# Fifteen small loads and eight early output stores on ScalarE's queue, in a decode kernel for gated attention and MLP

## The chip, the cores and the metric

The kernel runs on one core of a Trainium2 chip. The metric is the device time of one launch in microseconds (us): 1326.11 is the median of two runs before the change (1326.09 and 1326.12). The names of the engines are those of the profile: PE is TensorE (matmuls), DVE is VectorE, ACT is ScalarE, POOL is GpSimd, SP is SyncE, which here only issues DMAs. "SPq" and "ACTq" are the instructions with which SP and ACT issue DMAs.

## What is computed

Two rows (a batch of 2, one new token each) pass through attention over a cache of 16384 positions and, beside it, through a mixer with an MLP. A gate of each row mixes the two:

```python
g = sigmoid((x * gate_w).sum(-1, keepdims=True))
a = attention(x, k_cache, v_cache, wq, wo)     # B=2, 32 heads, Sk=16384, Dh=128
b = mixer_mlp(x, w1, w2, w3, w4)               # D=1024, F=3584
return g * a + (1 - g) * b                     # [2, 1, 1024], bf16
```

In the mixer a sequence of length 1 is shifted by one or two positions, so the operand of w2 is zero, and w1 isn't needed; the kernel multiplies a zeroed tile by w2. What has to be read is almost all cache: K and V are 2 x 32 x 16384 x 128 bf16 each, 268 MB apiece, of 570 MB in all.

## The kernel before

**The ring.** All large operands pass through one on-chip buffer, `ring`, of five slots, each 128 partitions by 32 KB. A K or V block of two heads takes two slots (8.4 MB), a half of a weight takes one. SP issues every one of these loads in one fixed order: wq (two halves, slots 0 and 1), w2 (slot 2), w3 (two halves, slots 3 and 4), w4 (two halves, slots 0 and 1 again), then K and V in turn for 32 pairs of heads (K in slots 3 and 4 or 2 and 3, V in 0 and 1), and wo at the end. Ahead of each load SP waits until the last matmul that reads the slot's earlier content is done; SP's queue is in order, so a load that waits holds those behind it.

**The prologue.** Each engine has one instruction list, emitted in program order. A wait is on a semaphore, and an instruction that waits holds all behind it on its engine. The steps ahead of the loop over head pairs are these:

- ACT loads the rows of x (L560) and of the gate vector (L561) into `xg_row`, and then, once POOL has cleared the tile `xrow`, x again into `xrow` in four pieces of two rows, at partitions 0 and 1, 32 and 33, and so on (L563). `xrow` is read at the end of the MLP only (L511).
- PE transposes `xg_row` (L583), and multiplies by wq (L604), which frees slots 0 and 1. DVE copies q out (L609, L616).
- The gate stage: DVE multiplies and sums (L393, L396), PE sums over partitions (the helper at L389), ACT takes a tanh (L399, preceded by ACT's table load), and DVE makes the gate and its complement from it (L400 to L406).
- The w2 stage: PE (L495), DVE (L531), PE (L537); DVE adds x (L481); the layer norm on DVE and PE, with one instruction on POOL (L430), gives `xn_bf` (L432).
- w3: 112 matmuls on each half (L466). The last of them frees slots 3 and 4, and SP may issue the first K load (L349).
- The gelu on DVE (L442 to L450) with a tanh on ACT (L448), then w4 on PE (L495), 56 matmuls for each half. The end of the second half frees slots 0 and 1 for the first V load (L353). DVE adds `xrow` and scales (L511, L513).

**The loop.** For each of the 32 pairs DVE transposes K in the ring (L647), PE makes the scores (L653), a softmax follows on DVE, PE and ACT (L663 to L680), PE multiplies by V (L689), and the result goes into a small tile (L698 to L703). Each pair's last reads of a slot release the next load into it.

**The end.** PE multiplies by wo (L726), DVE copies the two output rows into `orow` (L750), and SP and ACT store one row each (L752), and wait until it has landed.

`pl.dma(engine, fn, sem, waits)` puts a DMA on an engine's list and gives the event of its landing; `pl.add(engine, fn, waits)` puts any other instruction there.

Of the kernel before, what the change touches and what calls it, by code (L numbers as in the profile page):

```python
# [9 lines left out]
BF16 = mybir.dt.bfloat16  # L10
# [110 lines left out]
def build_kernel(nc, A_x, A_k, A_v, A_wq, A_wo, B_w1, B_w2, B_w3, B_w4, gate_w, out, dbg=None):  # L121
    dbg = dbg or {}
    B, Sq, D = A_x.shape
# [4 lines left out]
    P = 128  # L128
# [10 lines left out]
    NBD = D // P  # L139
# [19 lines left out]
    NQ = 4  # L159
    DQ = D // NQ  # L160
    PR = 32 * (NQ - 1) + 2
    assert DQ <= 512

    with ExitStack() as st:
        block = st.enter_context(nc.Block())
        sb = lambda name, shape, dt: st.enter_context(nc.sbuf_tensor(name, shape, dt))
# [34 lines left out]
        xrow = sb("xrow", [P, DQ], BF16)  # L201
        bgrow = sb("bgrow", [P, DQ], F32)
        orow = sb("orow", [P, DQ], BF16)
        m24 = sb("m24", [P, 2, NQ], F32)
        m2 = sb("m2", [P, 2], F32)
        gm = sb("gm", [P, 2], F32)
# [16 lines left out]
        sem = lambda n: st.enter_context(nc.semaphore(n))  # L223
# [3 lines left out]
        s_gw = sem("dgw")  # L227
        s_out = [sem(f"dout{i}") for i in range(2)]
        s_xr = sem("dxr")
        s_tail = [sem(f"dtl{i}") for i in range(len(wo_runs[1]))]  # L230
        pl = _Plan(esems)

# [37 lines left out]
        for hp in range(HP):  # L270
# [7 lines left out]
                    waits=(ev_rowm,), sig=True)  # L278
# [4 lines left out]
                        waits=(e0,), sig=True)  # L283
# [56 lines left out]
        def q_load(key):  # L340
            queue_load(key, wloads[key], (w_slots[n_w[0]],))
            n_w[0] += 1
# [219 lines left out]
        for qd in range(NQ):  # L562
            ev_xr = pl.dma("act", lambda e, qd=qd: e.dma_start(xrow[32 * qd:32 * qd + 2, :], A_x[:, 0, qd * DQ:(qd + 1) * DQ]), s_xr,  # L563
                           waits=(ev_xr0,))
        for hi in range(2):
            q_load(("wq", hi))
        for key in w_order:
# [14 lines left out]
        for nb in range(NBD):  # L582
            last = pl.add("pe", lambda e, nb=nb: e.transpose(tr_ps[:, nb * 4:nb * 4 + 3], xcols(xg_row, 3, nb), ident[0:3, 0:3]),  # L583
                          waits=(ev_x, ev_gw, ev_ident), sig=(nb == NBD - 1))
# [27 lines left out]
        for bp in range(NBP):  # L612
            evp = pl.add("pe", lambda e, bp=bp: e.matmul(q4_ps[:, bp, :], lhsT=PermQ[:, bp, :],
                                                        rhs=q_sb[:, :, :].rearrange("p h b -> p (h b)"), start=True, stop=True),
                         waits=(ev_q, ev_const, ev_r0), sig=(bp == NBP - 1))
# [135 lines left out]
        for b, eng in enumerate(("sp", "act")):  # L751
            ev_out = pl.dma(eng, lambda e, b=b: e.dma_start(out[b, 0, :].rearrange("(q n) -> q n", q=NQ), orow[b:PR:32, :]), s_out[b],  # L752
                            waits=(ev_fin,))
# [28 lines left out]
def bass_gated_mix__mha_block_cached__mixer_s_mlp__decode_kernel(  # L782
    nc: bass.Bass,
    A_x: bass.AP,
    A_k_cache: bass.AP,
    A_v_cache: bass.AP,
    A_wq: bass.AP,
    A_wo: bass.AP,
    B_x: bass.AP,
    B_w1: bass.AP,  # L790
    B_w2: bass.AP,
    B_w3: bass.AP,
    B_w4: bass.AP,
    gate_w: bass.AP,
    out: bass.AP,
):
    build_kernel(nc, A_x, A_k_cache, A_v_cache, A_wq, A_wo, B_w1, B_w2, B_w3, B_w4, gate_w, out)
# [28 lines left out]
```

## Time and profile before

| | |
|---|---|
| median of the two runs | 1326.11 us |
| the profiled execution's own time | 1325.93 us |
| its span, first to last instruction | 1324.1 us |
| PE busy | 785.1 us (59%) |
| DVE busy | 657.2 us (50%) |
| ACT busy | 45.7 us (3%) |
| DMA traffic | 570.60 MB, mean 431 GB/s |

One execution was recorded by the hardware profiler. Times in its views are counted from the start of the span. A row of the timeline has the start, the busy time, the engine, the line of the kernel, the operation, the tiles written and read, and the count of instructions that were merged into the row; in brackets stands how long the engine had been idle and what ended that. A row of the waits has the waiting line, the line waited for, the total, the count and the longest. A row of a DMA queue has its packets, megabytes, and the time that its packets took as a share of the 16 DMA engines' time in the window asked for (packets are counted by their starts, so a short window can show over 100%). q1 and q10 are the queues of SP and of ACT.

### The profile page before, as it was taken

Reading aid. Unit: us, or ns where it says so; the run is one execution under the profiler, and the core shown is the slowest. Engines: PE = TensorE matmul, PEld = TensorE weight load, DVE = VectorE, ACT = ScalarE, POOL = GpSimd, SP = SyncE. Lnnn points to the kernel's source line nnn. Section 1 sums busy time; section 2 is a strip of 40 time slices with the busy share of each in tenths; the row PEclk is TensorE's granted clock in tenths of the full one; section 3 lists DMA queues with packets and bytes.
Section 4 is the critical chain, followed back from the end, with each engine's and each line's share of the span. In section 5 each row is a group of like instructions: output and inputs, shape, how many; then the busy total and the mean of one; then the engine's idle time right before and its main releaser. Section 6 shows DMA issues by size and latency. Waiting matters only on the chain.

```text
span 1324.1 us, 12290 instructions
## 1 busy us (share of the span) xinstructions
PE 785.1 (59%) x5235; PEld 335.8 (25%) x5235; DVE 657.2 (50%) x523; ACT 45.7 (3%) x99; POOL 23.5 (2%) x110
## 2 busy tenths in 40 slices
PE   3645557656556765555676555566655456665646
PEld 2512223222222322222232222222222222222223
DVE  1054446655444665544466554446655444665543
ACT  0000000000000000000000000000000000000000
POOL 3000000000000000000000000000000000000000
PEclk9966787777678777767877776788787788878679
DMA  9999999999999999999999999999999999999998
GB/s 403 445 424 434 436 434 434 432 438 432 430 440 432 430 440 430 430 440 430 434 436 430 438 434 436 432 432 438 434 428 440 432 430 440 430 432 438 430 434 359
DMA packets 11138, 570.60 MB, mean 431 GB/s; under 512 B 1252, under 2 KB 1268, under 8 KB 1655
## 3 DMA queue, kind: packets, MB, share of 16 engines
q1 hardware_dynamic: 11096, 570.43, 99.7%
q8 instruction: 8, 0.13, 0.0%
q10 hardware_dynamic: 30, 0.01, 0.0%
q14 instruction: 4, 0.02, 0.0%
HBM read 570.44 MB, written 0.00 MB: 431 GB/s over the span
## 4 chain that ended last, share of the span: by engine, by line
DMA 70%; PE 23%; DVE 6%; issue 0%; SPq 0%
DMA ring<-in_A_k_cache_dram 65%; PE ps L653 23%; DVE ring L647 6%; DMA ring<-in_B_w_dram 3%; DMA ring<-in_A_wo_dram 2%; PE ps L466 1%; SPq L324 0%; DVE orow L750 0%; PE ps L726 0%
## 5 line engine op out<-in xcount | busy, mean ns | idle before, releaser
L653 PE MATMUL ps<-ring,Z 128*128 128x512 bf16 x2048 | 534.5, 420 | 389.1 <-DVE ring L647 388.5
L647 DVE STREAM_TRANSPOSE ring<-ring 128x2048 f32<-128x2048 f32 x256 | 565.2, 2275 | 278.6 <-DMA ring<-in_A_k_cache_dram 278.6
L653 PEld LDWEIGHTS ps<-ring,Z 128*128 128x128 bf16 x2048 | 204.4, 104 | 706.7 <-issue 473.5
L689 PE MATMUL ps<-ring,PT_sb 128*32 128x512 bf16 x2048 | 168.2, 501 | 4.1 <-DVE recip L680 3.7
L703 DVE SCALAR_TENSOR_TENSOR OT_sb<-ps,gT,recip 128x2 f32 x32 | 7.0, 220 | 203.4 <-PE ps L700 203.4
L689 PEld LDWEIGHTS ps<-ring,PT_sb 128*32 128x32 bf16 x2048 | 67.6, 122 | 90.8 <-issue 69.6
L674 ACT ACTIVATE P_sb<-ps,negm 128x512 bf16<-128x512 f32 x32 | 22.0, 687 | 1013.9 <-DVE negm L672 1013.9
L663 DVE TENSOR_REDUCE rA<-ps 128x1 f32<-128x512 f32 x32 | 22.1, 692 | 64.1 <-PE ps L653 64.1
L678 PE MATMUL ps<-rowsum,hsel 128*128 128x1 f32 x128 | 24.0, 291 | 37.9 <-ACT P_sb L674 37.9
L676 DVE STREAM_TRANSPOSE PT_sb<-P_sb 128x512 bf16<-128x512 bf16 x32 | 22.8, 711 | 27.0 <-ACT P_sb L674 27.0
L634 POOL TENSOR_TENSOR Z<-q_f,mask 128x8 bf16<-128x8 f32 x64 | 12.3, 227 | 1214.3 <-PE ps L653 1214.3
L678 PEld LDWEIGHTS ps<-rowsum,hsel 128*128 128x128 f32 x128 | 21.3, 236 | 40.7 <-ACT P_sb L674 40.7
L665 PE MATMUL ps<-ident,rmax_bf 128*1 128x128 bf16 x32 | 6.9, 217 | 33.1 <-DVE rmax_bf L664 33.1
L698 ACT ACTIVATE acc_sb<-ps 128x512 bf16<-128x512 f32 x32 | 19.1, 597 | 198.8 <-PE ps L689 198.8
L700 PE MATMUL ps<-dsel,acc_sb 128*128 128x2 bf16 x128 | 8.1, 167 | 22.5 <-ACT acc_sb L698 22.5
L466 PE MATMUL ps<-xn_bf,ring 128*128 128x2 bf16 x224 | 14.5, 202 | 2.9 <-DMA ring<-in_B_w_dram 2.9
L466 PEld LDWEIGHTS ps<-xn_bf,ring 128*128 128x128 bf16 x224 | 14.4, 172 | 3.0 <-DMA ring<-in_B_w_dram 3.0
L700 PEld LDWEIGHTS ps<-dsel,acc_sb 128*128 128x128 bf16 x128 | 5.3, 96 | 38.2 <-ACT acc_sb L698 38.2
L665 PEld LDWEIGHTS ps<-ident,rmax_bf 128*1 128x1 bf16 x32 | 2.5, 79 | 48.9 <-DVE rmax_bf L664 48.9
L604 PE MATMUL ps<-xT_bf,ring 128*128 128x2 bf16 x256 | 7.1, 165 | 11.7 <-DVE xT_f L588 7.4
L666 DVE TENSOR_REDUCE m_sb<-ps 1x2 bf16<-1x128 bf16 x32 | 8.9, 278 | 9.9 <-PE ps L665 9.9
L672 DVE TENSOR_SCALAR negm<-ps,cAB 128x1 f32<-128x1 f32 x32 | 8.9, 277 | 9.2 <-PE ps L669 9.2
(97 smaller groups left out, 85.8 us busy)
## 6 DMA issues: line engine op xcount, KB each, us to landing
ring<-in_B_w_dram SPq DMA_DIRECT2D x4, 3584.0 KB, 35.4
ring<-in_A_wq_dram SPq DMA_DIRECT2D x2, 4096.0 KB, 17.5
ring<-in_A_wo_dram SPq DMA_DIRECT2D x1, 4096.0 KB, 40.2
ring<-in_B_w_dram SPq DMA_DIRECT2D x1, 2048.0 KB, 27.1
ring<-in_A_wo_dram SPq DMA_DIRECT2D x1, 2048.0 KB, 22.2
ring<-in_A_wo_dram SPq DMA_DIRECT2D x1, 1024.0 KB, 24.4
ring<-in_A_k_cache_dram SPq DMA_DIRECT2D x32, 26.8
ring<-in_A_v_cache_dram SPq DMA_DIRECT2D x32, 29.2
```

What stands on the lines that cost most here:

```text
L466: fn = lambda e, nb=nb, kl=kl: e.matmul(out_ps[:, nb, :], lhsT=cols(wv, kl, nb, nout), rhs=rhs_of(k0 + kl), start=False, stop=True, skip_g ...
L634: ev = pl.add("pool", lambda e, hp=hp: e.tensor_tensor(Z[:, :, ZO:ZO + P].rearrange("p t (i c) -> p t i c", c=32)[:, :, 2 * hp:2 * hp + 2, ...
L647: return pl.add("dve", lambda e: e.transpose(ap, ap), waits=(arrived(("k", n)),), sig=True)
L653: ev = pl.add("pe", lambda e, bp=bp: e.matmul(S_ps[:, 0:NCOL], lhsT=Z[:, bp, ZO - 2 * u:ZO - 2 * u + P], rhs=kv[:, :, bp // 2, :, bp % 2], ...
L663: e1 = pl.add("dve", lambda e: e.tensor_reduce(rA[:, :], S_ps[:, 0:NCOL], axis=AX.X, op=ALU.max), waits=(ev_S[n],), sig=True)
L665: e3 = pl.add("pe", lambda e: e.transpose(mt_ps, rmax_bf[:, :], ident[:, :]), waits=(e2,), sig=True)
L674: e7 = pl.add("act", lambda e: e.activation(P_sb[:, :], S_ps[:, 0:NCOL], ACT.Exp, bias=negm[:, 0:1], scale=scale, accum_out=rowsum[:, 0:1] ...
L676: e8 = pl.add("dve", lambda e: e.transpose(PT_sb[:, :], P_sb[:, :]), waits=(e7,), sig=True)
L678: e9 = pl.add("pe", lambda e, hp=hp: e.matmul(l_ps[:, hp:hp + 1], lhsT=hsel[:, hp, :], rhs=rowsum[:, 0:1], start=True, stop=True, skip_gro ...
L689: ev = pl.add("pe", lambda e, jj=jj, cg=cg: e.matmul(acc_ps[32 * cg:32 * cg + 32, 0:512], lhsT=PT_sb[:, 32 * jj:32 * jj + 32], rhs=vv[:, 4 ...
L698: e1 = pl.add("act", lambda e: e.activation(acc_sb[:, :], acc_ps[:, 0:512], ACT.Copy), waits=(ev_pv,), sig=True)
L700: e2 = pl.add("pe", lambda e, w=w: e.matmul(oT_ps, lhsT=acc_sb[:, w * P:(w + 1) * P], rhs=dsel[:, w, :], start=(w == 0), stop=(w == 3)), w ...
```

## The change

After ACT's four loads into `xrow`, and ahead of ACT's first activation in program order, the change puts on ACT's list:

- fifteen loads of 1, 2, ... 15 rows, of 16 bytes each, from the gate vector into a new tile `small` that nothing reads, all on one new semaphore and without waits of their own;
- a wait until all fifteen have landed;
- eight stores from `xrow` into the second output row, each waiting until the one before has landed (the first until `xrow` is loaded). Four shapes, each twice: 4 rows of 512 bytes, 2 rows of 512 bytes, 128 rows of 16 bytes, 16 rows of 128 bytes. The final store at L752 writes that output row again;
- a wait until the last of the eight has landed.

The list of no other engine is changed.

```diff
+        small = sb("small", [16, 16, 8], BF16)
...
+        s_small = sem("dsmall")
+        s_early = sem("dearly")
...
         for qd in range(NQ):
             ev_xr = pl.dma("act", lambda e, qd=qd: e.dma_start(xrow[32 * qd:32 * qd + 2, :], A_x[:, 0, qd * DQ:(qd + 1) * DQ]), s_xr,
                            waits=(ev_xr0,))
+        for k in range(1, 16):
+            ev_small = pl.dma("act", lambda e, k=k: e.dma_start(small[0:k, k, :], gate_w[0:8 * k].rearrange("(k c) -> k c", k=k)), s_small,
+                              waits=())
+        o1 = out[1, 0, :]
+        early = [lambda e: e.dma_start(o1.rearrange("(q n) -> q n", q=NQ), xrow[1:PR:32, :]),
+                 lambda e: e.dma_start(o1[0:2 * DQ].rearrange("(q n) -> q n", q=2), xrow[1:34:32, :]),
+                 lambda e: e.dma_start(o1.rearrange("(p r) -> p r", p=P), xrow[:, 0:NBD]),
+                 lambda e: e.dma_start(o1.rearrange("(p r) -> p r", p=16), xrow[0:16, 0:D // 16])]
+        pl.add("act", lambda e: e.wait_ge(ev_small.sem, ev_small.val))
+        ev_early = ev_xr
+        for fn in early * 2:
+            ev_early = pl.dma("act", fn, s_early, waits=(ev_early,))
+        pl.add("act", lambda e: e.wait_ge(ev_early.sem, ev_early.val))
         for hi in range(2):
             q_load(("wq", hi))
```

## The prediction

> **What bounds the kernel now.** I read the page first (its DMA queues and the engine shares of its chain), then the chain in order of time over the first 140 us, then the instructions of SyncE (SP), TensorE (PE), ScalarE (ACT) and VectorE (DVE) there, and last the DMA queues in short windows. From the page:
>
> ```profile
> q1 hardware_dynamic: 11096, 570.43, 99.7%
> ...
> q10 hardware_dynamic: 30, 0.01, 0.0%
> ...
> DMA 70%; PE 23%; DVE 6%; issue 0%; SPq 0%
> ```
>
> q1 carries SP's big loads and takes 99.7% of sixteen engines over the whole span: the kernel is bound by bytes, and only an idle stretch of that queue makes it longer. q10 is ScalarE's: 15 rows (2 of x, 1 of the gate, 8 into xrow, 4 of the output) made its 30 packets, so a row counts twice: its data, and a completion behind it.
>
> So the question is whether the change ever leaves q1 without work. The early chain says where that could be:
>
> ```profile
> 2.80 43.19 DMA ring<-in_B_w_dram
> ...
> 46.04 7.28 PE ps L466 x112
> ...
> 53.33 29.03 DMA ring<-in_A_k_cache_dram
> ```
>
> The first K load (K0) is issued at 53.33, and the next view names what releases it. SP's instructions, its wait, and PE's:
>
> ```profile
> 53.33 0.33 SPq L349 DMA_DIRECT2D ring<-in_A_k_cache_dram  x1
> 66.27 0.33 SPq L353 DMA_DIRECT2D ring<-in_A_v_cache_dram  x1
> 94.89 0.33 SPq L349 DMA_DIRECT2D ring<-in_A_k_cache_dram  x1
> ```
> ```profile
> SPq L349 <- PE ps L466: 25.4, 1, 25.4
> ```
> ```profile
> 37.53 7.26 PE L466 MATMUL ps<-xn_bf,ring 128*128 128x2 bf16 x112 [1.61 <-DMA ring<-in_B_w_dram]
> 46.04 7.26 PE L466 MATMUL ps<-xn_bf,ring 128*128 128x2 bf16 x112 [1.25 <-DMA ring<-in_B_w_dram]
> 55.41 3.15 PE L495 MATMUL ps<-ring,GT_bf 128*2 128x256 bf16 x56 [2.11 <-DVE GT_bf L450]
> 63.06 3.15 PE L495 MATMUL ps<-ring,GT_bf 128*2 128x256 bf16 x56 [4.50 <-DMA ring<-in_B_w_dram]
> 84.83 15.26 PE L653 MATMUL ps<-ring,Z 128*128 128x512 bf16 x56 [18.61 <-DVE ring L647]
> ```
>
> K0 must wait for the last w3 matmul (L466), which frees its ring slots. When it is issued, w4 is still flowing: its second half releases PE at 63.06. From then until 82.36 (53.33 + 29.03) q1 moves K0 alone. So K0 has cover: it could be issued some 9 us later before q1 runs dry.
>
> Upstream of L466 stands ScalarE, with one tanh in the gate stage:
>
> ```profile
> 1.33 0.24 ACTq L561 DMA_DIRECT2D xg_row<-in_gate_w_dram  x1
> 15.22 1.15 ACTq L563 DMA_DIRECT2D xrow<-in_A_x_dram  x4
> 16.41 1.28 ACT L399 ACT_TABLE_LOAD   x1 [16.41 <-issue]
> 29.93 0.17 ACT L399 ACTIVATE th<-ps 128x2 f32<-128x2 f32 x1 [12.24 <-PE ps L389]
> ```
> ```profile
> 30.14 0.17 DVE L400 TENSOR_SCALAR gT<-th 128x2 f32<-128x2 f32 x1 [0.88 <-ACT th L399]
> ...
> 31.75 1.22 DVE L531 TENSOR_TENSOR hsd<-ps,mask 128x1024 bf16<-128x1024 f32 x1 [0.99 <-PE ps L495]
> ```
>
> ScalarE idles 12.24 us ahead of that tanh. DVE works in program order, so L531 and the layer norm behind L400, and by them L466 and K0, all stand behind the tanh although they don't use its result.
>
> **The change: fifteen loads.** Everything added sits on ScalarE's queue between L563 and L399, so it starts at 16.4. Four issues in L563 took 1.15, or 0.29 each; fifteen take 4.3, to 20.7, inside the idle time. What costs is the wait for them. What a small transfer meets beside q1 is shown by the existing ones: the queues in the windows 16.4 to 19.3, 19.3 to 24.8, 25 to 27 and 30 to 50, and PE's first wait:
>
> ```profile
> q1 hardware_dynamic: 32, 1.05, 84.2%
> q14 instruction: 1, 0.01, 0.7%
> ```
> ```profile
> q1 hardware_dynamic: 127, 2.34, 99.7%
> q8 instruction: 1, 0.02, 1.1%
> q10 hardware_dynamic: 16, 0.00, 0.3%
> ```
> ```profile
> q1 hardware_dynamic: 63, 0.99, 115.2%
> ```
> ```profile
> q1 hardware_dynamic: 330, 8.54, 99.5%
> ```
> ```profile
> 8.11 0.63 PE L583 MATMUL ps<-ident,xg_row 3*128 3x3 bf16 x8 [8.11 <-DMA xg_row<-in_gate_w_dram]
> ```
>
> The xrow loads were issued from 15.22 on, yet no q10 packet starts before 19.3; then all 16 (8 rows, 8 completions) start by 24.8. In those 5.5 us q1 moved 127 packets, 7.9 on each engine. If each two-row load uses the same two engines, each of these had 8 small packets: one small packet for each big one, in turn. That is my price: **a small packet costs one big packet's time on its engine**. From 25 to 27 that is 2 × 16 / 63 = 0.51 us, from 30 to 50 it is 20 × 16 / 330 = 0.97 us.
>
> Loads of 1 to 15 rows have 120 rows. If they all start at the same engine, it has fifteen rows, 30 packets, behind the xrow packets that end at 24.8. 2.2 us at 0.51 pass 4.3 of them, the other 25.7 cost 24.9: done at 51.9. The lower end, the rows spread evenly over sixteen engines (15 packets each), gives 27 + 10.7 × 0.97 = 37.4. I take the upper one, since the xrow count fits only if loads share their engines. The q1 bytes themselves are hardly slowed: 16 small packets took 0.3% of that window.
>
> **Eight stores in a chain.** Each is issued only when the one before has landed. Under load the nearest rows are the gate row, issued at 1.33 and in PE's hands at 8.11 (6.8), and xrow's first load, issued at 15.22, starting at 19.3 (4.1 later), its completion one big packet of 32 KB (1.05 MB / 32) behind, which takes 1.2 at one engine's 27 GB/s from 30 to 50 (8.54 MB / 20 us / 16): 5.3. I take 5.5. Without load it is the final output store:
>
> ```profile
> 1321.88 0.64 SPq L752 DMA_DIRECT2D out_dram<-orow  x1
> ```
> ```profile
> SPq L164 <- DMA out_dram<-orow: 1.0, 1, 1.0
> ```
>
> 0.64 + 1.0 = 1.64. From 51.9 the first store lands at 57.4, the second at 62.9, and there q1 has run dry, since K0 isn't issued. Six more at 1.64 are 9.8: 72.7. Two of the six are cut into 128 rows of 16 bytes and two into 16 rows of 128, which no row shows; they cannot be cheaper than the 512-byte rows by more than 1.64 each, and dearer up to the loaded 5.5.
>
> Then L399. Its table load, 1.28, stood under the idle time; behind the added waits it is bare: tanh at 74.0. (By the Trainium skill, page "ScalarE: Activation LUTs", section "What ACT_TABLE_LOAD costs", such a load is about 2.7 us; the row here says 1.28, and the measured one is used; by the page the sum would be 1.4 more.)
>
> **From the tanh to the DMA queue.** Before, 29.93 to 53.33 was 23.4. Two waits in it go, as their producers are long done: 0.99 (L531 on PE) and 1.25 (L466 on w3's second half). So 21.2, and K0 is issued at 95.2. Could PE be slower after 40 idle us? A later stage with the same 256-column rows as L495:
>
> ```profile
> 1313.70 1.92 PE L726 MATMUL ps<-ring,OT_sb 128*2 128x256 bf16 x64 [0.42 <-DVE OT_sb L718]
> ```
>
> 30 ns each there, 56 in L495: the early stage already ran at about half pace, so I add nothing. Bounds: twice L466's 14.5 (+14.5), or half of it (−7.3).
>
> How long does q1 take to restart? SP's first issue, and bytes moved from 1 to 8 us in slices of 0.175:
>
> ```profile
> 0.74 0.87 SPq L324 DMA_DIRECT2D ring<-in_A_wq_dram  x2
> ```
> ```profile
> GB/s 0 0 0 12 1135 1498 0 0 187 0 187 0 0 0 749 936 749 562 0 0 0 562 1123 936 374 0 0 0 562 1123 948 374 0 0 0 562 1123 936 375 0
> ```
>
> Bytes flow from about 1.7, so 1.0. w4's last packets leave some 0.5 before PE's 63.06. q1 is empty from 62.5 to 96.2: **33.7 us**.
>
> Is it given back? V0 was issued 12.94 after K0, 4.50 of it waiting for w4, which is there now; at 95.2 + 8.4 = 103.6 it is ahead of K0's end near 116, so V0 stays hidden. K1 comes 12.5 after K0 lands, as before (94.89 − 82.36), under V0's flow. From there everything runs as before, 33.7 later, at a q1 share that leaves nothing to catch up with. The final two stores are untouched.
>
> Sum: the profiled execution, 1325.93 (span 1324.1), + 33.7 = 1359.6; the median 1326.11 is 0.2 higher. **Forecast 1360.**
>
> **Rivals.** *Not slower.* The small transfers slip past at their unloaded price: loads done at 20.7 + 1.64, stores + 13.1, table load + 1.28: tanh at 36.7, K0 at 57.9, before q1 runs dry: 1326. The slip must stay below about 8 us at K0 (tanh before 40.3). For it speaks how little q10 moves; against it the empty 4 us ahead of 19.3 and PE's 8.11. Chance 7%.
>
> *The loads drain in groups.* If an engine takes all waiting small packets at one turn, the loads are done near 27; six stores at 5.5 land by 60.0, the seventh near 63.5, the eighth at 65.1, tanh 66.4: 7.6 earlier, 1352, on the edge of 2%. The Trainium skill states such a rule in "DMA: Bandwidth & Descriptors", section "Queues, rings and completion order": an engine drains a packet of about 9 to 17 descriptors from one ring before it switches. The 16 packets stretched over 5.5 us speak against it here. The even spread above lies between: stores at 42.9, 48.4, 53.9, 59.4 and 63.3, three more, tanh 69.5: 1355. Chance of the group rule 14%.
>
> *Dearer stores.* If the six late ones cost a loaded 5.5 each, tanh is at 97.2 and the time 1383; if only the two with 16-byte rows do, 2 × 3.9 more: 1367; with a half-speed L466 alone, 1374. No row shows such writes. Chance 18%.
>
> **How the numbers follow.** The forecast with its lower wing (1354 to 1364) has 57%, the rivals 7, 14 and 18, and 4 are left for what I haven't seen. The range 1350 to 1374 leaves out the first rival, the far half of the dear stores and some of the rest. The 2% line, about what a measurement can tell from no change, is at 1352.6: slower has the 57, the 18 and half of the 14: 0.82. Within 2%: the other half, the 7 and what is left: 0.16. Faster 0.02: nothing on the chain is shortened but waits that are repaid.
>
> **What will show it.** tanh L399 near 74 and K0's issue near 95; a hole in the DMA row from about 62.5 to 96; in ScalarE's queue eight spaced stores, two wide and six narrow; q10 packets in the windows 25 to 52 thinned one to one with q1's. It is wrong if K0 is issued before 62, if the loads land long before 50, or if a later stage shifts by another amount than the hole.

## The result, and the profile after

The changed kernel takes 1360.8 us (median of two runs, 1360.58 and 1361.01) against 1326.11: a ratio of 1.0262, 95% interval 1.0245 to 1.0279, so it is slower by more than 2%. The profiled execution took 1360.58, its span 1358.8. The forecast was 1360, in a range of 1350 to 1374.

Line numbers are 3 higher than before ahead of the added block and 16 higher behind it (in the experiments the second step differs). The page shows the same bytes over more time, and far more packets on ScalarE's queue q10 (packets, megabytes, share of 16 engines):

```profile
DMA  9829999999999999999999999999999999999998
...
q1 hardware_dynamic: 11096, 570.43, 97.2%
...
q10 hardware_dynamic: 646, 0.03, 0.0%
```

The row of DMA digits cuts the span into 40 slices of 34 us. The hole begins in the second (the "8") and fills most of the third (the "2", 68 to 102); nothing like it follows. 97.2% of 1358.8 and 99.7% of 1324.1 are nearly the same busy time (1321 and 1320): the bytes did not get dearer, q1 stood still. DMA in the window that holds the hole:

```profile
DMA packets 376, 0.07 MB, mean 2 GB/s; under 512 B 365, under 2 KB 373, under 8 KB 373
```

From 62.7 to 94.3 all queues together moved 0.07 MB. The chain in order of time names what fills that stretch and what came ahead of it (start, us, what):

```profile
21.60 32.30 DMA small<-in_gate_w_dram
53.92 6.31 DMA out_dram<-xrow
60.25 3.40 DMA out_dram<-xrow
...
79.10 14.34 PE ps L469 x224
93.46 23.09 DMA ring<-in_A_k_cache_dram
```

ScalarE's timeline has the whole added block:

```profile
16.43 5.58 ACTq L569 DMA_DIRECT2D small<-in_gate_w_dram  x15
53.92 0.62 ACTq L572 DMA_DIRECT2D out_dram<-xrow  x1
60.25 0.51 ACTq L573 DMA_DIRECT2D out_dram<-xrow  x1
63.68 0.39 ACTq L574 DMA_DIRECT2D out_dram<-xrow  x1
65.15 0.33 ACTq L575 DMA_DIRECT2D out_dram<-xrow  x1
66.49 0.56 ACTq L572 DMA_DIRECT2D out_dram<-xrow  x1
68.14 0.52 ACTq L573 DMA_DIRECT2D out_dram<-xrow  x1
69.70 0.35 ACTq L574 DMA_DIRECT2D out_dram<-xrow  x1
71.14 0.32 ACTq L575 DMA_DIRECT2D out_dram<-xrow  x1
71.55 1.28 ACT L402 ACT_TABLE_LOAD   x1 [71.55 <-DMA out_dram<-xrow]
72.84 0.17 ACT L402 ACTIVATE th<-ps 128x2 f32<-128x2 f32 x1
```

Fifteen loads are issued by 22.0 and waited for until 53.9. Two stores are spaced wide, 6.3 and 3.4, and the rest follow at about 1.5. The tanh comes at 72.84 instead of 29.93. DVE waits for it, and PE for DVE:

```profile
73.05 0.17 DVE L403 TENSOR_SCALAR gT<-th 128x2 f32<-128x2 f32 x1 [43.67 <-ACT th L402]
```
```profile
79.10 14.33 PE L469 MATMUL ps<-xn_bf,ring 128*128 128x2 bf16 x224 [1.35 <-DVE xn_bf L435]
```

Both halves of w3 now run in one piece, since both had long landed. SP's queue and the transposes of the first K block on DVE:

```profile
93.46 0.33 SPq L352 DMA_DIRECT2D ring<-in_A_k_cache_dram  x1
```
```profile
116.57 4.51 DVE L663 STREAM_TRANSPOSE ring<-ring 128x2048 f32<-128x2048 f32 x2 [13.34 <-DMA ring<-in_A_k_cache_dram]
```

Before, that transpose started at 82.38 (53.33 + 29.03, and a step of 0.02), so the first K block is 34.2 late. The second K block is issued 33.6 late (128.51 for 94.89), and the whole span is 34.7 longer: nothing of note is given back.

### The profile page after: what moved, and what is told of

It reads as the page before. It is cut to its first block, busy times and chain, and to the rows that moved or that the text cites. A ratio compares the mean times of both kernels' runs of the same rounds, so it can differ in the third digit from the quotient of the medians.

```text
span 1358.8 us, 12315 instructions
## 1 busy us (share of the span) xinstructions
PE 781.2 (57%) x5235; PEld 333.2 (25%) x5235; DVE 656.8 (48%) x523; ACT 45.7 (3%) x99; POOL 23.6 (2%) x110
## 3 DMA queue, kind: packets, MB, share of 16 engines
q1 hardware_dynamic: 11096, 570.43, 97.2%
## 4 chain that ended last, share of the span: by engine, by line
DMA 69%; PE 23%; DVE 6%; POOL 1%; issue 1%; ACTq 0%; SPq 0%; ACT 0%; POOLq 0%
DMA ring<-in_A_k_cache_dram 63%; PE ps L669 22%; DVE ring L663 5%; DMA small<-in_gate_w_dram 2%; DMA ring<-in_A_wo_dram 2%; DMA out_dram<-xrow 1%; PE ps L469 1%; ACTq L569 0%; POOL esel L246 0%; SPq L327 0%; ACT L402 0%; POOL PermQ L246 0%; PE ps L392 0%; DVE hsd L534 0%; ACTq L566 0%
## 5 line engine op out<-in xcount | busy, mean ns | idle before, releaser
L469 PE MATMUL ps<-xn_bf,ring 128*128 128x2 bf16 x224 | 14.3, 202 | 1.4 <-DVE xn_bf L435 1.4
L469 PEld LDWEIGHTS ps<-xn_bf,ring 128*128 128x128 bf16 x224 | 14.3, 165 | 1.4 <-issue 1.4
```

What stands on the lines that cost most here:

```text
L469: fn = lambda e, nb=nb, kl=kl: e.matmul(out_ps[:, nb, :], lhsT=cols(wv, kl, nb, nout), rhs=rhs_of(k0 + kl), start=False, stop=True, skip_g ...
```

## The experiments

Each kernel is the changed one with the edit shown; lines that are removed or added are against it. "The time" is one run beside a run of the kernel before (1325.99 to 1326.10 in these series), except where an interval is given.

### The loads alone

The eight stores are left out, and the wait for them.

```diff
-        ev_early = ev_xr
-        for fn in early * 2:
-            ev_early = pl.dma("act", fn, s_early, waits=(ev_early,))
-        pl.add("act", lambda e: e.wait_ge(ev_early.sem, ev_early.val))
```

> Leaves out the eight stores and the wait for them. My theory (30 small packets take turns with the big packets of q1 on the busiest engine): the wait for the loads ends where it did with the whole change, near 53.9, the bare table load puts the tanh at 55.2, and the time is 1326.1 plus what the tanh lies behind 38.6 (72.8 less the 34.2 that the whole change cost): 1343. Rival (the chain of stores is the cost, the loads land early once nothing waits behind them): about 1326.

The time was 1340.65. ScalarE:

```profile
30.21 1.28 ACT L402 ACT_TABLE_LOAD   x1 [30.21 <-PE ps L392]
53.24 0.17 ACT L402 ACTIVATE th<-ps 128x2 f32<-128x2 f32 x1 [21.75 <-DMA small<-in_gate_w_dram]
```

The loads land near 53.2 with nothing behind them, so the wait is theirs. The table load was already done at 31.5: it runs ahead of the activation's last wait, not behind it, where the expectation of 1343 had put it. Of the 2 us by which 1343 was too high, 1.3 are the table load, and 0.7 that the loads landed at 53.2 and not at 53.9 (14.6 behind 38.6 makes 1340.7).

### Fifteen loads of one row

```diff
-            ev_small = pl.dma("act", lambda e, k=k: e.dma_start(small[0:k, k, :], gate_w[0:8 * k].rearrange("(k c) -> k c", k=k)), s_small,
+            ev_small = pl.dma("act", lambda e, k=k: e.dma_start(small[0:1, k, :], gate_w[0:8].rearrange("(k c) -> k c", k=1)), s_small,
```

The stores are left out too.

> Fifteen loads of one row each instead of 1 to 15 rows, and no stores. Theory (the busiest engine counts): all fifteen rows are on the first engine, again 30 packets there, so the wait ends near 53.9 and the time is 1343, as with 120 rows. Rival (the whole number of small packets counts, 30 here against 240): the wait ends near 28, the tanh comes in time, 1326.

The time was 1339.59.

```profile
52.16 0.17 ACT L402 ACTIVATE th<-ps 128x2 f32<-128x2 f32 x1 [20.69 <-DMA small<-in_gate_w_dram]
```

One eighth of the rows, and the wait is 1.1 us shorter. The number of rows in all is not what costs. The queues from 30 to 50 show what does:

```profile
q1 hardware_dynamic: 330, 8.54, 99.3%
...
q10 hardware_dynamic: 21, 0.00, 0.1%
```

The record does not name a packet's engine. But each of the sixteen engines moved 330 / 16 = 20.6 packets of q1 in this window, and the loads put 21 of theirs between them: that is one small packet for each one of q1, on one engine alone.

### One load of 120 rows

```diff
-        for k in range(1, 16):
-            ev_small = pl.dma("act", lambda e, k=k: e.dma_start(small[0:k, k, :], gate_w[0:8 * k].rearrange("(k c) -> k c", k=k)), s_small,
+        ev_small = pl.dma("act", lambda e: e.dma_start(small[0:120, :], gate_w[0:960].rearrange("(k c) -> k c", k=120)), s_small,
```

The tile is [120, 8] for it; the stores are left out.

> One load of 120 rows of 16 bytes and the wait for it, in place of the fifteen loads of 1 to 15 rows (120 rows too) and of the stores. Theory (turns on the busiest engine): the rows spread evenly, eight on an engine and one completion, nine turns, some 6 to 7 us behind the last xrow packets on the engines that carry these: the wait ends near 31, tanh near 31 to 32, inside the cover, 1326. Rival (every row costs, wherever it lies): near 53 as with fifteen loads, 1341.

The time was 1326.53.

```profile
31.70 0.17 ACT L402 ACTIVATE th<-ps 128x2 f32<-128x2 f32 x1 [0.35 <-DMA small<-in_gate_w_dram]
```

The same 120 rows in one transfer land 21.5 us earlier than in fifteen, at the time that nine turns give. The time is 0.5 above that of the kernel before.

### Ten loads, and six

```diff
-        for k in range(1, 16):
+        for k in range(1, 11):
```

and `range(1, 7)`; the stores are left out in both.

> Loads of 1 to 10 rows alone, no stores (the run with all fifteen alone: tanh at 53.2, 1340.7). Theory: ten packets fewer on the busiest engine, each a turn of 1.07: tanh near 42.6, 1330. Rival (the rows count, 55 instead of 120): tanh near 37.4, in time for the first K load, 1326.

> Loads of 1 to 6 rows alone. Theory: nine packets' pairs fewer than fifteen loads on the busiest engine, tanh near 34 to 35, ahead of the edge at 38.6: 1326, nothing lost, although the tanh is 4 to 5 us late. Rival (each us by which the tanh is late is lost): 1330 to 1331.

The times were 1331.17 and 1326.36. The tanh, first with ten loads, then with six:

```profile
43.83 0.17 ACT L402 ACTIVATE th<-ps 128x2 f32<-128x2 f32 x1 [12.36 <-DMA small<-in_gate_w_dram]
```
```profile
35.08 0.17 ACT L402 ACTIVATE th<-ps 128x2 f32<-128x2 f32 x1 [3.74 <-DMA small<-in_gate_w_dram]
```

From six to ten loads the tanh moves by 8.75, from ten to fifteen by 9.41: with two packets a load on the busiest engine, 1.09 and 0.94 each, where 0.97 was priced. And the cover is real: a tanh 5.2 us late (35.08 for 29.93) costs 0.3, no more than two runs of one kernel can differ by (1360.58 and 1361.01), and one that is 13.9 late costs 5.2. The edge lies between, where the theory has it (38.6, or 8.7 late).

### The stores alone

The loads and the wait for them are left out.

```diff
-        for k in range(1, 16):
-            ev_small = pl.dma("act", ...
...
-        pl.add("act", lambda e: e.wait_ge(ev_small.sem, ev_small.val))
```

> Leaves out the fifteen loads and the wait for them. Theory: the chain starts when xrow has landed, near 24, and meets q1 at work for its first five stores: 5.5 to 6.3 each, but the store of 128 rows takes some 14, as it has nine packets on each engine; the fifth lands near 61, the last three cost about 1.5 each, the tanh comes near 68: 1356. Rival (costs add up): the loads' share goes, 17 us, and 1344 is left. Rival (a store costs the same whatever its rows): tanh near 65.7, 1353, and the third store is no longer than the others in the trace.

The time was 1354.51, the tanh at 66.86. The first five stores:

```profile
25.22 0.60 ACTq L569 DMA_DIRECT2D out_dram<-xrow  x1
31.94 0.51 ACTq L570 DMA_DIRECT2D out_dram<-xrow  x1
38.11 0.39 ACTq L571 DMA_DIRECT2D out_dram<-xrow  x1
51.21 0.33 ACTq L572 DMA_DIRECT2D out_dram<-xrow  x1
57.66 0.56 ACTq L569 DMA_DIRECT2D out_dram<-xrow  x1
```

Beside q1 a store of a few rows takes 6.2 to 6.7 (the fifth, 4.5, met q1 as it ran dry) and the one of 128 rows 13.1 (38.11 to 51.21). That is what turns demand: from 38.0 to 51.3 q10 had 144 packets, 128 rows and 16 completions, or nine on each engine if they are spread evenly; a store of a few rows has two on its engines, and seven more at 0.97 are 6.8. The time lies halfway between 1356 and the last rival's 1353; it is the third store, twice as long as the others, that speaks against that rival. In the full change the same shape, with q1 dry, takes 1.47 (63.68 to 65.15). The costs do not add: loads alone 14.6, stores alone 28.5, both 34.7, because stores that start late find an idle DMA.

### The wait for the loads moved behind the stores

```diff
-        pl.add("act", lambda e: e.wait_ge(ev_small.sem, ev_small.val))
         ev_early = ev_xr
         for fn in early * 2:
             ev_early = pl.dma("act", fn, s_early, waits=(ev_early,))
         pl.add("act", lambda e: e.wait_ge(ev_early.sem, ev_early.val))
+        pl.add("act", lambda e: e.wait_ge(ev_small.sem, ev_small.val))
```

> All loads and stores as in the change, but the wait for the loads stands behind the stores. Theory: the first store's rows are queued behind the loads on the same engines, so it lands near 55.5 although it is issued near 25; the second lands near 62, the rest as before, tanh near 71.2: 1359, so that wait is nearly free to take away. Rival (only the wait holds the stores back): as with the stores alone, 1354.5.

The time was 1359.18.

```profile
24.91 0.61 ACTq L572 DMA_DIRECT2D out_dram<-xrow  x1
55.00 0.51 ACTq L573 DMA_DIRECT2D out_dram<-xrow  x1
```

The first store is issued 29 us earlier and lands only 5.3 earlier (55.0 for 60.25): it stands behind the loads in the same queue. Removing that wait by itself is worth 1.6.

### Stores that do not wait for each other

The eight stores are 4 rows of 64 bytes each, into separate parts of the output row.

```diff
+        o4 = out[1, 0, :].rearrange("(q n) -> q n", q=NQ)
+        for k in range(8):
+            ev_early = pl.dma("act", lambda e, k=k: e.dma_start(o4[:, 32 * k:32 * k + 32], xrow[1:PR:32, 32 * k:32 * k + 32]), s_early,
+                              waits=(ev_xr,))
-        for fn in early * 2:
-            ev_early = pl.dma("act", fn, s_early, waits=(ev_early,))
```

> Fifteen loads and the wait for them as in the change; the eight stores are 4 rows of 64 bytes each into separate parts of the output row, and none waits for another; one wait behind the last. Theory: they are issued within 4 us of 53.9, run in turns with q1 until it is dry near 62.5, and the wait ends near 63.5; tanh near 64.8, 1353. Rival (each store's landing in memory costs, chain or not): 1361.

The time was 1352.58.

```profile
53.98 4.46 ACTq L574 DMA_DIRECT2D out_dram<-xrow  x8
58.53 1.28 ACT L402 ACT_TABLE_LOAD   x1 [58.53 <-issue]
65.13 0.17 ACT L402 ACTIVATE th<-ps 128x2 f32<-128x2 f32 x1 [5.32 <-DMA out_dram<-xrow]
```

Taking the chain away is worth 8.2 of the 34.7 (the stores' shapes changed with it), between five and six idle landings of 1.5.

### The table loaded early

```diff
+        pl.add("act", lambda e: e.activation(warm[:, :], neg_half[:, :], ACT.Tanh, scale=0.5), waits=(ev_const,))
         for k in range(1, 16):
```

> The change with a tanh of a constant tile ahead of the added block, so that the table load runs at 16.4. Theory: the 1.28 of the table load goes from behind the last store, 1359.5. Rival (the table load is hidden anyway, or comes again): 1360.8.

The time was 1360.89 (four runs, 1360.64 to 1361.02; ratio to before 1.0264, interval 1.0246 to 1.0281): no difference from the change. The second store's issue, the third's, the last's, and the tanh:

```profile
59.22 0.51 ACTq L575 DMA_DIRECT2D out_dram<-xrow  x1
64.02 0.39 ACTq L576 DMA_DIRECT2D out_dram<-xrow  x1
...
71.47 0.32 ACTq L577 DMA_DIRECT2D out_dram<-xrow  x1
72.82 0.17 ACT L403 ACTIVATE th<-ps 128x2 f32<-128x2 f32 x1 [54.91 <-DMA out_dram<-xrow]
```

The last store takes 1.35 from issue to landing. In the change it was issued at 71.14 and so landed near 72.5, while the table load ran from 71.55 to 72.83 beside it. No more than 0.35 of the table load was bare, and in this run the second store landed 0.34 later than in the change (64.02 for 63.68) and took that back.

### The block moved behind the last tanh of the prologue

The same loads, stores and waits stand after `for run in pro_stages: run()`.

> The same loads, stores and waits, but behind the last tanh of the prologue on ScalarE's queue, where ScalarE was idle for 49 us before its first exponential at 104. Theory: behind w4 the big packets are those of K and V, 64 KB, and a turn costs 2.4 us; the loads land only near 119, about when q1 runs dry for want of the first softmax, the eight stores then cost some 12, the exponential starts near 132 to 134 instead of 104, and V of the second pair is issued some 29 late, of which about 20 are lost: 1346. Rival (ScalarE's idle time hides them there): 1326.

The time was 1349.66. ScalarE's first load issues, first store, last store and first exponential:

```profile
54.47 5.28 ACTq L739 DMA_DIRECT2D small<-in_gate_w_dram  x15
120.13 0.60 ACTq L742 DMA_DIRECT2D out_dram<-xrow  x1
...
130.90 0.32 ACTq L745 DMA_DIRECT2D out_dram<-xrow  x1
132.41 0.69 ACT L677 ACTIVATE P_sb<-ps,negm 128x512 bf16<-128x512 f32 x1 [77.70 <-DMA out_dram<-xrow]
```

Here the loads took 65.7 us to land (54.47 to 120.13), against 37.5 in the change, since most of the packets that they alternate with are K's and V's, 64 KB each. Idle time of ScalarE did not hide them: its first exponential came 28 us late (132.41 for 104.19), and 23.6 of it were lost.

### All waits moved to the end

The loads, and the stores of the run without a chain, stay in place; both waits stand near the end of ScalarE's list, ahead of its final store.

```diff
-        pl.add("act", lambda e: e.wait_ge(ev_small.sem, ev_small.val))
...
-        pl.add("act", lambda e: e.wait_ge(ev_early.sem, ev_early.val))
...
+        pl.add("act", lambda e: e.wait_ge(ev_small.sem, ev_small.val))
+        pl.add("act", lambda e: e.wait_ge(ev_early.sem, ev_early.val))
         ev_alast = do_aproj()
```

> The fifteen loads and the eight separate stores of the run without a chain, issued at the same place, but both waits stand at the end of ScalarE's list, ahead of the final store. Theory: the transfers themselves cost nothing, only ScalarE's wait for them ahead of the tanh: 1326. Rival (the small packets slow q1 itself, or the stores to memory do): some us above 1326.

The time was 1327.81, 1.7 above the kernel before. PE's second w3 half, and DVE's first transpose:

```profile
47.02 7.26 PE L469 MATMUL ps<-xn_bf,ring 128*128 128x2 bf16 x112 [2.30 <-DMA ring<-in_B_w_dram]
```
```profile
84.17 17.66 DVE L657 STREAM_TRANSPOSE ring<-ring 128x2048 f32<-128x2048 f32 x8 [14.61 <-DMA ring<-in_A_k_cache_dram]
```

The waits carry nearly all of the cost, but not all of it: q1's own loads land later, w3's second half by 1.0 (47.02 for 46.04) and the first K block by 1.8 (84.17 for 82.38). My theory had nothing there. Not all of the 1.8 need be the small packets' doing. The trace has each packet's start and length, and where one starts as another ends, the two can be put on one engine. Read so, K0 ended last, at 83.64, on an engine that also had a 16 KB packet of q8 (which the profile calls "instruction") at 67.66; the others had ended it by 83.00, and all of them by 81.94 in the kernel before. So some 0.6 hangs on which engine that packet met. What the rest, about 1.1, is made of, no run here separates.

## Why the prediction was right

**The place.** The claim was that the tanh holds DVE, DVE holds L466 (now L469) and that holds K0, with some 8 us of cover at K0. The after-trace shows each link, and the six-load and ten-load runs show both sides of the cover's edge. Beyond it the cost follows the tanh: 38.6 is taken from the change alone, and in all eight kernels here with a tanh from 43.83 to 72.84 the profiled time is 1326.1 plus what the tanh lies behind 38.6, within 0.35. The prediction had that edge at 40.3, 1.7 too late, mostly for the restart (below).

**The price of a turn.** A small packet was priced at one big packet of its engine, 0.97 us from 30 to 50. The loads ended at 53.9 where 51.9 was expected; 0.4 of that lies between the start of the last small packet (53.54) and ScalarE's next issue (53.92), the rest was not taken apart. The queues of the change from 44.8 to 53.6 show the tail of it:

```profile
q1 hardware_dynamic: 147, 3.76, 99.3%
q10 hardware_dynamic: 17, 0.00, 0.1%
```

In 8.8 us each engine moved 9.2 packets of q1. By their starts the 17 small packets run in two files (48.19 and 48.22, 49.25 and 49.28, and so on), so two engines are left with loads, and that is about one small packet for each one of q1. The group rule of the Trainium skill (page "DMA: Bandwidth & Descriptors", section "Queues, rings and completion order") would have had the loads done near 27; no run here agrees with it: they ended at 53.2 alone, and moved by 0.94 to 1.09 for each packet added on the busiest engine.

**The stores.** 5.5 each was expected for the first two, and 6.31 and 3.40 came: the second, issued at 60.25, met q1 as it ran dry. For the six idle ones 9.8 was expected; from 63.68 to a landing near 72.5 they took 8.8. The unknown shapes are no dearer than the known: 128 rows of 16 bytes took 1.47 from issue to next issue, 4 rows of 512 bytes 1.65 (66.49 to 68.14).

**The table load.** "Behind the added waits it is bare" is the step that failed. It was put at 1.28 and cost at most 0.35, for it runs ahead of the activation's last wait: it stood behind seven of the stores, but beside the eighth. It had run ahead before the change too: the row quoted in the prediction has it at 16.41, 13.5 us ahead of its tanh, and I read past that.

**From the tanh to K0** 21.2 was expected, 20.6 measured: L469 took 14.33 in one piece instead of two times 7.26, and PE's wait ahead of it was 1.35 and not 1.61.

**The restart** was mis-sized. 33.7 late had K0 landing at 116.1, 20.9 behind its issue at 95.2. It was issued at 93.46 and took 23.09, 2.2 more. The bytes did begin within 1.0; but the first round of 64 KB packets, from 94.3 to 97.4, was slower than later ones, by the queue in that window and from 100 to 110:

```profile
q1 hardware_dynamic: 16, 1.05, 102.4%
```
```profile
q1 hardware_dynamic: 71, 4.65, 107.8%
```

From these shares, 16 packets took 3.17 us each (102.4% of 3.1 us on 16 engines), and the 71 later ones 2.43. On the slowest engine the first took 3.5, so this is about 1.1 of the 2.2. Most of the rest is another queue's packet, from 102 to 104:

```profile
q8 instruction: 1, 0.02, 2.8%
```

By starts and ends of packets, as above, it held one engine for 0.88, and the K0 packet behind it took 2.97: that engine ended K0 at 116.03, the other fifteen by 115.06. In the kernel before, such a packet at 67.78 met an engine that had begun K0 2 us ahead of the last one (60.53 for 62.59), and delayed nothing. The prediction had no term for either. What makes the first round slow was not tried; the run with the loads alone has it too (2.6 to 3.6 for its first packets).

So the tanh was 1.2 early (loads +2.0, first two stores −1.3, the six −1.0, table load −0.9), K0's issue another 0.6, and the restart gave back 2.2. That a forecast came within 1 us although its terms were off by up to 2.2 is luck: they cancelled.

**The rivals.** That small transfers slip past (1326) fell with the run of loads alone; that they drain in groups (1352) fell by the 0.94 to 1.09 us for each packet added. Dear stores did not come; the stores that are dear are those beside q1 (13.1 for 128 rows), and in the change only the first two, of 4 and 2 rows, met q1.

## What to carry to other kernels

Where one queue keeps the DMA engines full, the price of a small transfer is set by the packet size of its neighbour and by the count of rows and completions on its busiest engine, not by its bytes: fold small loads into one that spreads over the engines, and never let an in-order engine wait for them ahead of work that others stand behind. Before pricing such a wait, find how late the held work may be (here 8.7 us), as anything within that cost at most 0.5 here and all beyond it cost in full. Moving the same block into another idle stretch can make it dearer, if the packets there are larger.

## What the runs showed that was not expected

- The table load runs ahead of its activation's last wait: at 30.21 for a tanh at 53.24, at 58.53 for one at 65.13.
- 128 rows of 16 bytes go to memory in 1.47 us when the DMA engines are idle, and in 13.1 beside q1.
- With nobody waiting for the small transfers the kernel was still 1.7 us above the one before; how much of that is theirs stays open.
- One 16 KB packet of q8 can delay a large load by 1.0 us (116.03 for 115.06) or by nothing, depending on the engine that it meets.
- The profile shows a granted clock of 1.00 from the start on, but the trace's first clock record is at 66.9, and at 99.9 in the change: ahead of that, 1.00 stands for no record. The matmuls have the true pace. Those of L498 in the change start in groups of four, 0.21 us apart up to 99.9 and 0.11 from there on, 53 and 27 ns each, so the early stage runs at half pace, as the prediction took it to. All of L495 in the kernel before ended at 66.2 and ran at 56. In the change the row's 5.34 for 112, 48 ns, is a mean of the two:

```profile
95.54 5.34 PE L498 MATMUL ps<-ring,GT_bf 128*2 128x256 bf16 x112 [2.11 <-DVE GT_bf L453]
```
